# One core of Trainium2: banded attention and a rational-function MLP, with the first tile's loads put first, its masks applied from PSUM and the weights' low bits taken in place

## The chip, the cores and the metric

The kernel runs on one core of one Trainium2 chip. A core has five engines, each with its own queue that it works off in order: TensorE (PE, matrix products, from SBUF into PSUM), VectorE (DVE), ScalarE (ACT), GpSimd (POOL) and SyncE (SP), which here only issues DMA transfers. Engines wait for each other by semaphores. The metric is the device time of one execution in microseconds. Before the change it is 999.59 us, the median of three runs (999.03 to 999.78).

## The reference

Inputs are q, k, v of shape 8 x 8 x 576 x 64 (batch, heads, sequence, head size), w_in 512 x 2048, w_out 2048 x 512, and the coefficients a (four) and b (two).

```
scores = q @ k^T / sqrt(64) - slope[h] * |i - j|       where 0 <= i - j < 128, else -1e9
attn   = exp(scores - max);  attn = attn / (sum + 1e-9)
x      = (attn @ v) as 4608 rows (batch, position) x 512 (head, size)
h      = x @ w_in
g      = (a0 + a1 h + a2 h^2 + a3 h^3) / (1 + |b0| |h| + |b1| h^2 + 1e-6)
out    = g @ w_out
```

All values are float32.

## The kernel before

**Tiles.** The 4608 rows are 36 blocks of 128, two blocks a tile, 18 tiles. For each tile the attention of its 256 rows gives x, the MLP's up-projection runs over 16 chunks c of 128 hidden columns (h), the rational function turns h into g, and the down-projection adds g times the chunk's rows of w_out into two accumulators (acc). Attention comes in half-tiles: step j belongs to tile j // 2 and holds two pairs of heads, i = 0 and 1. Steps 0 and 1 make tile 0's x.

**Attention of one step.** For each pair one DMA brings keys and queries (kq), two bring values (v), all on SP. PE forms scores, those of the window's own positions in a main bank (sc) and the rest in a side bank; DVE merges the two with a predicated copy, then adds the bias and takes the maximum (L507, out pr and st), ACT takes exp (L512), DVE the reciprocal of the sum (L520), POOL multiplies by it (L521). PE transposes pr into PSUM (pt for tile 0, otherwise back into sc), ACT or DVE copies all 512 columns to p_all (L539), and POOL splits what the two blocks of keys share: p_far = p_all times a mask (L543), p_all minus p_far (L544). Then PE multiplies both by v (the values), and ACT or DVE copies the result to x_hi (L413 for tile 0, L415 after).

**Weights.** w_in and w_out arrive as 8-byte words, two 32-bit halves an element; a load brings one chunk of one matrix (raw, 32 loads of 128 x 512 words, in buffers that are later reused). The float32 weight is put together from three results: ACT's Prelu on the upper half (L582), the top three bits of the lower half, taken by ACT or by DVE into the PSUM tile cv (L583), and a shift and an OR on DVE (L584), which gives w32. Tile 0 multiplies in plain float32 with w32. For the later tiles each weight is split into hi, a rounded copy by ACT (L596), and lo, the rest, by DVE or POOL (L597); a product is then three faster matmuls. PSUM holds four buffers under the tag h, shared by h, side, pt, the values' px, cv and the warm-up.

**Rational function.** ACT takes |h| (L635) and a linear term (L638, or L649 after tile 0), POOL forms the denominator (L636 a multiply and add, then a product), ACT logarithm and exp, DVE four or more products (L640 to L647 for tile 0).

**Order.** All work is entered as operations with a due time and the engines that may do it, with a cost in ns for each. A planner (class Plan) goes through time, gives every free engine the ready operation of least due time, and so fixes each engine's queue; the engines then run these queues in order, whatever the real times are. Due times come from one table of numbers (A0, DA, T0, ... in the body of banded_attention_ratio_mlp). The DMA queue of ACT carries the constants (masks16, bias_first, id_sb, bias_std, ab), SP's all other transfers. At the start PE runs seven wide and eight narrow matmuls on constants (L713, L715), before and between the first scores.

Of the kernel before, what the change touches and what calls it, by code (L numbers as in the profile page):

```python
# [79 lines left out]
class Plan:  # L80
# [34 lines left out]
    def order(self):  # L115
# [76 lines left out]
        while n < total:  # L192
# [12 lines left out]
            for e in "pavgsq":  # L205
                while free_at[e] <= t:
# [7 lines left out]
                    if best is None:  # L214
                        break
# [54 lines left out]
def banded_attention_ratio_mlp(ctx: ExitStack, tc: tile.TileContext, kqv, w_in, w_out, ab, bias, ident, out):  # L270
# [87 lines left out]
    def job(j, i):  # L358
# [60 lines left out]
    def attention(j):  # L419
# [4 lines left out]
        side = [slot(ps4, [P, 2, 2, P], F32, f"side{h}", tag="h") for h in range(2)]  # L424
# [6 lines left out]
        extra = lambda h: ap(side[h])[:, 0].rearrange("q i (b c) -> q i b c", b=2)  # L431
# [35 lines left out]
        for h in range(2):  # L467
            plan.op(A + 0.5, {"v": dve(4 * P)}, lambda e, h=h: nc.vector.copy_predicated(
                out=main(h).rearrange("q i b (k c) -> q (i b) k c", k=2),
                mask=halves(ap(masks)[:, 0].bitcast(U32))[:, None].to_broadcast([P, 4, 2, 64]),  # L470
                data=extra(h).rearrange("q i b c -> q (i b) c")[:, :, None].to_broadcast([P, 4, 2, 64])),
                reads=[mk[h], (side[h], 0), (masks, 0)], writes=[mk[h]])
# [10 lines left out]
    def unit(j, i, A, main, mk, pt, v):  # L483
# [54 lines left out]
        plan.op(A + D2, {"p": 28 + 108 * 4}, transpose, reads=[(pr, y) for y in range(4)] + [(id_sb, 0)], writes=pk)  # L538
        plan.op(A + D2 + 0.2, {"a": act(4 * P, 1), "v": dve(4 * P)} if j < 3 else {"a": act(4 * P, 1)}, lambda e: (nc.scalar.copy if e == "a" else nc.vector.tensor_copy)(ap(w)[:, : 4 * P].rearrange("q (k h c) -> q k h c", k=2, h=2), pt()), reads=pk, writes=[(w, 0)])  # L539
        mixed = lambda: ap(w).rearrange("q (k r) -> q k r", k=2)[:, :, : 2 * P].rearrange("q k (h c) -> q k h c", h=2)[:, :, :, :64]  # L540
        far = lambda: ap(masks)[:, 1].rearrange("q (k c) -> q k c", k=2)[:, :, None].to_broadcast([P, 2, 2, 64])
# [20 lines left out]
    def convert(k):  # L562
# [18 lines left out]
        plan.op(T - WL, {"s": 1600}, load, writes=[(raw, 0), (raw, 1)], after=1000 * (T - WL - 4), follows=[raws[k - NL]] if k >= NL else ())  # L581
        plan.op(T, {"a": 575}, lambda e: nc.scalar.activation(top().bitcast(F32), top().bitcast(F32), AF.Prelu, scale=2.0**-112, alpha=-(2.0**32)), writes=[(raw, 0)])  # L582
        plan.op(T, {"a": 640, "v": 603}, lambda e: nc.scalar.activation(cv(), low().bitcast(U32), AF.Relu, bias=low_bias, scale=2.0**-29) if e == "a" else nc.vector.tensor_single_scalar(cv(), low(), 29, op=ALU.logical_shift_right), reads=[(raw, 1)], writes=[ck])  # L583
        plan.op(T + 1, {"v": 603}, lambda e: nc.vector.scalar_tensor_tensor(ap(bits).bitcast(I32), top(), 3, cv(), ALU.logical_shift_left, ALU.bitwise_or), reads=[(raw, 0), ck], writes=[(bits, 0)])  # L584
# [18 lines left out]
    def mlp(t, cs):  # L603
# [32 lines left out]
        plan.op(E, {"g": tsc}, lambda e: nc.gpsimd.tensor_scalar(v(g_q), v(g_u), ap(babs)[:, 1:2], ap(babs)[:, 0:1], ALU.mult, ALU.add), reads=[(g_u, 0), (babs, 0)], writes=[(g_q, 0)])  # L636
# [75 lines left out]
    for j in range(7):  # L712
        plan.op(-9, {"p": 216}, lambda e, j=j: nc.tensor.matmul(ap(warm), ones[:, :P], ones, start=(j == 0), stop=(j == 6)), writes=[(warm, 0)], after=600)  # L713
    for j in range(8):
        plan.op(-9, {"p": 108}, lambda e: nc.tensor.matmul(ap(warm)[:, :256], ones[:, :P], ones[:, :256], start=True, stop=True), writes=[(warm, 0)], after=3617.319 + 500.0 * j)  # L715
# [66 lines left out]
```

## Time and profile before

| | |
|---|---|
| median of three runs | 999.59 us |
| the profiled execution, its time | 999.67 us |
| its span, first to last instruction | 997.9 us |
| busy: PE, DVE, ACT, POOL | 976.8, 791.6, 611.6, 525.4 us |
| mean granted clock of PE | 0.991 |
| moved by DMA | 73.86 MB |

The span is what the trace covers; the execution's own time is 1.8 us more. Two rows of the page show the course, in 40 slices of 25 us, each digit the busy tenths of a slice: PE, and the DMA engines.

```profile
PE   6899899999999999999999999999999999999998
DMA  9991311121112112121212131203021221200000
```

PE is full nearly everywhere but in the first four slices; DMA is full in the first three, while the weights come in. A wait is shown behind a row in square brackets: how long the engine stood idle before it, and who ended that.

### The profile page before, as it was taken

To read this page: it belongs to the slowest core of one execution; us is meant where nothing else is said; L and a number is where in the kernel's file an instruction comes from. 1 tells how busy PE (TensorE), PEld (TensorE's weight loads), DVE (VectorE), ACT (ScalarE), POOL (GpSimd) and SP (SyncE) were. 2 spreads that over 40 slices of the span, in tenths; PEclk is the share of its full clock that TensorE was granted. 3 is DMA by queue.
4 is the path that set the end of the run, shared out by engine and by line. 5 is a ranking of instruction groups with operands and counts; after the bars stand their busy time and mean duration, and the time that the engine had idled before them with its cause. 6 is when DMAs were issued, how large, how long until landed. Compare 5 with 4: busy or idle time off the path is not lost.

```text
span 997.9 us, 25220 instructions
## 1 busy us (share of the span) xinstructions
PE 976.8 (98%) x9999; PEld 867.0 (87%) x9999; DVE 791.6 (79%) x1786; ACT 611.6 (61%) x1410; POOL 525.4 (53%) x529
## 2 busy tenths in 40 slices
PE   6899899999999999999999999999999999999998
PEld 4756698999999999999999999999999999999997
DVE  5799997887878787877787877878787878777775
ACT  5798865665656566655656565656566565656452
POOL 3448984555555554554545454555555545545332
PEclk7899999999999999999999999999999999999999
DMA  9991311121112112121212131203021221200000
GB/s 283 366 325 26 95 48 60 50 94 41 62 51 74 56 54 70 49 75 55 70 49 75 39 96 45 79 2 102 22 80 44 55 75 54 71 1 22 2 22 22
DMA packets 54502, 73.86 MB, mean 74 GB/s; under 512 B 5488, under 2 KB 38512, under 8 KB 54384
## 3 DMA queue, kind: packets, MB, share of 16 engines
q1 hardware_dynamic: 53664, 71.59, 22.9%
q8 instruction: 79, 1.29, 0.6%
q10 hardware_dynamic: 720, 0.66, 0.2%
q14 instruction: 39, 0.32, 0.1%
HBM read 62.79 MB, written 9.44 MB: 72 GB/s over the span
## 4 chain that ended last, share of the span: by engine, by line
PE 91%; DVE 3%; DMA 3%; ACT 1%; issue 1%; SPq 0%; ACTq 0%; DVEq 0%
PE h L621 40%; PE acc L676 39%; PE side L397 5%; PE sc L536 3%; PE sc L444 3%; PE side L444 1%; DMA v<-in_kqv 1%; DVE w L584 1%; DMA kq<-in_kqv 1%; DMA raw<-in_w_in 1%; DMA bias_std<-in_bias 1%; ACT pr L512 0%; DVE cv L583 0%; DVE g_q L644 0%; DVE g L647 0%
## 5 line engine op out<-in xcount | busy, mean ns | idle before, releaser
L621 PE MATMUL h<-x_hi,hi 128*128 128x256 f32 x1088 | 313.6, 288 | 0.0
L621 PE MATMUL h<-x_hi,lo 128*128 128x256 f32 x1088 | 306.2, 281 | 0.0
L621 PE MATMUL h<-x_lo,hi 128*128 128x256 f32 x1088 | 306.0, 281 | 0.0
L636 POOL TENSOR_SCALAR g_q<-g_u,babs 128x512 f32<-128x512 f32 x144 | 123.2, 855 | 252.8 <-ACT g_u L635 252.1
L621 PEld LDWEIGHTS h<-x_lo,hi 128*128 128x128 f32 x1088 | 204.7, 188 | 43.1 <-issue 1.0
L621 PEld LDWEIGHTS h<-x_hi,hi 128*128 128x128 f32 x1088 | 205.3, 189 | 25.4 <-issue 0.7
L676 PE MATMUL acc<-lo,g_h 128*128 128x512 f32 x544 | 214.7, 395 | 0.0
L676 PE MATMUL acc<-hi,g_h 128*128 128x512 f32 x544 | 214.5, 394 | 0.0
L676 PE MATMUL acc<-hi,g_l 128*128 128x512 f32 x544 | 207.7, 400 | 0.0
L621 PEld LDWEIGHTS h<-x_hi,lo 128*128 128x128 f32 x1088 | 204.9, 188 | 0.0
L650 POOL TENSOR_TENSOR g_q<-g_q,g_u 128x512 f32<-128x512 f32 x136 | 175.9, 1293 | 11.0
L521 POOL TENSOR_TENSOR pr<-pr,st 128x512 f32<-128x512 f32 x72 | 76.0, 1055 | 178.8 <-DVE st L520 128.6
L656 DVE SCALAR_TENSOR_TENSOR g_h<-h,ab_sb,g_u 128x512 fp32r<-128x512 f32 x136 | 101.9, 749 | 80.4 <-ACT g_u L654 79.4
L653 ACT ACTIVATE g_u<-g_q,fixed 128x512 f32<-128x512 f32 x136 | 98.0, 720 | 90.8 <-POOL g_q L650 90.7
L512 ACT ACTIVATE pr<-pr,st 128x128 f32<-128x128 f32 x288 | 112.6, 392 | 48.7 <-DVE st L507 48.7
L635 ACT ACTIVATE g_u<-h 128x512 f32<-128x512 f32 x144 | 86.0, 597 | 59.6 <-PE h L621 56.2
L649 ACT ACTIVATE g_p<-h,ab_sb 128x512 f32<-128x512 f32 x136 | 105.5, 778 | 18.0 <-PE h L621 17.9
L651 DVE TENSOR_TENSOR g_p<-h,g_p 128x512 f32<-128x512 f32 x136 | 93.7, 689 | 27.2 <-ACT g_p L649 23.4
L657 DVE SCALAR_TENSOR_TENSOR g_q<-g_q,g_h 128x512 f32<-128x512 f32 x136 | 97.7, 718 | 12.8
L658 DVE SCALAR_TENSOR_TENSOR h<-h,ab_sb,g_q 128x512 f32<-128x512 f32 x136 | 102.9, 756 | 3.5
L676 PEld LDWEIGHTS acc<-hi,g_h 128*128 128x128 f32 x544 | 102.6, 189 | 2.1
L652 DVE SCALAR_TENSOR_TENSOR h<-g_p,ab_sb,h 128x512 f32<-128x512 f32 x136 | 102.1, 751 | 2.5 <-ACT g_u L635 0.3
(75 smaller groups left out, 1516.6 us busy)
## 6 DMA issues: line engine op xcount, KB each, us to landing
kq<-in_kqv SPq DMA_DIRECT2D x72, 320.0 KB, 3.8
v<-in_kqv SPq DMA_DIRECT2D x144, 128.0 KB, 3.9
out<-o SPq DMA_DIRECT2D x34, 256.0 KB, 2.0
raw<-in_w_in SPq DMA_DIRECT2D x16, 512.0 KB, 8.6
raw<-in_w_out SPq DMA_DIRECT2D x16, 512.0 KB, 8.6
bias_t<-in_bias SPq DMA_DIRECT2D x44, 64.0 KB, 2.0
out<-o SPq DMA_DIRECT2D x4, 128.0 KB, 1.8
bias_first<-in_bias ACTq DMA_DIRECT2D x1, 256.0 KB, 4.6
```

Of the source, the lines that this page charges most:

```text
L512: nc.scalar.activation(ap(pr)[:, :, y, :], ap(pr)[:, :, y, :], AF.Exp, bias=ap(st)[:, y : y + 1], scale=-1.0, accum_out=ap(st)[:, 4 + y : ...
L621: nc.tensor.matmul(h(n), w[:, k, :], x[:, k, :], start=(k == 0 and m == 0), stop=(k == NKC - 1 and m == len(seq) - 1))
L636: plan.op(E, {"g": tsc}, lambda e: nc.gpsimd.tensor_scalar(v(g_q), v(g_u), ap(babs)[:, 1:2], ap(babs)[:, 0:1], ALU.mult, ALU.add), reads=[ ...
L649: plan.op(E, {"a": act(W, 1, 2) - 20}, lambda e: nc.scalar.activation(v(g_p), v(h_s), AF.Identity, bias=ap(ab_sb)[:, 2:3], scale=ap(ab_sb) ...
L650: plan.op(E, {"g": ttc}, lambda e: nc.gpsimd.tensor_tensor(v(g_q), v(g_q), v(g_u), ALU.mult), reads=[(g_q, 0), (g_u, 0)], writes=[(g_q, 0) ...
L651: plan.op(E, {"v": dve(W)}, lambda e: nc.vector.tensor_tensor(v(g_p), v(h_s), v(g_p), ALU.mult), reads=[(h_s, 0), (g_p, 0)], writes=[(g_p, ...
L652: plan.op(E, {"v": dve(W, 1)}, lambda e: stt(v(h_s), v(g_p), ap(ab_sb)[:, 1:2], v(h_s), ALU.add, ALU.mult), reads=[(h_s, 0), (g_p, 0), (ab ...
L653: plan.op(E, {"a": act(W, 0, 1)}, lambda e: nc.scalar.activation(v(g_u), v(g_q), AF.Ln, bias=guard, scale=1.0), reads=[(g_q, 0)], writes=[ ...
L656: plan.op(E, {"v": dve(W, 1)}, lambda e: stt(v(g_h), v(h_s), ap(ab_sb)[:, 0:1], v(g_u), ALU.add, ALU.mult), reads=[(h_s, 0), (g_u, 0), (ab ...
L657: plan.op(E, {"v": dve(W)}, lambda e: stt(v(g_q), v(g_q), GUARD, v(g_h).bitcast(F32), ALU.add, ALU.mult), reads=[(g_q, 0), (g_h, 0)], writ ...
L658: plan.op(E, {"v": dve(W, 1)}, lambda e: stt(v(h_s), v(h_s), ap(ab_sb)[:, 0:1], v(g_q), ALU.add, ALU.subtract), reads=[(h_s, 0), (g_q, 0), ...
L676: nc.tensor.matmul(ap(accs[t][i]), x[:, sl], w, start=(c == 0 and part == 0 and m == 0), stop=(c == NFC - 1 and part == parts - 1 and m == ...
```

## The change

Four things are done, and the table of due times is new.

1. *Loads of tile 0 first.* All four kq and then all eight v loads of tile 0 are put ahead of every other transfer of SP; tile 1's kq and v move behind five weight loads. On ACT's DMA queue bias_std goes ahead of id_sb. The two side banks of step 0 are used by step 1 too, in their other half.
2. *Masks from PSUM.* For steps 0 to 4 (DIRECT = 5) ACT copies only half of the transposed columns (L566), and DVE makes the other two products straight from PSUM: p_all times the new mask `near`, which is the far mask with its column halves swapped (L567), and p_far (L568). POOL does neither. In steps 0 and 1 the multiplication by st may go to DVE (L541).
3. *TensorE's gaps filled.* The fifteen warm-up matmuls become as many narrow ones as the planner finds idle time for, from 0.6 to 24.352 us.
4. *Low bits in place.* The lower halves are reduced to their top bits where they lie, by POOL (minimum and multiply) or by ACT (L611); cv and its PSUM buffers go, and DVE's shift and OR (L612) reads both operands from SBUF.

In tile 1 ACT may also do the denominator's multiply and add.

```diff
+DIRECT = 5
...
                     if best is None:
-                        break
+                        if e != "p" or self.fill is None or not self.fill[0] <= t < self.fill[1] or self.fill[2].turn is None:
+                            break
+                        o, spot = Op(), self.fill[2]
+                        o.due, o.engines, o.emit, o.after, o.rows, o.sb = 0.0, {"p": 108}, self.fill[3], 0.0, 1.0, False
...
-    A0, DA, T0, L0, L1 = -4.313, 1.223, 17.768, 62.357, 26.153
+    A0, DA, T0, L0, L1 = -15.22, 0.8197, 19.751, 66.839, 26.934
...
+        for k in range(2):
+            c, o = slice(64 * k, 64 * k + 64), slice(64 - 64 * k, P - 64 * k)
+            plan.op(-7, {"v": 140}, lambda e, c=c, o=o: nc.vector.tensor_copy(ap(near)[:, c], ap(masks16)[:, 1, o]), reads=[(masks16, 0)], writes=[(near, k)])
...
-        plan.op(u0 - JL, {"s": 1.6 * N}, lambda e: eng[e].dma_start(ap(kq), src[:, :N]), writes=[(kq, 0)], after=late)
+        plan.op(u0 - JL if t else 2 * j + i - 19, {"s": 1150}, lambda e: eng[e].dma_start(ap(kq), src[:, :N]), writes=[(kq, 0)], after=late)
...
+        if j < DIRECT:
...
+            plan.op(T, {"a": act(2 * P, 1)}, lambda e: nc.scalar.copy(fresh(1), picked(1)), reads=pk, writes=[(w, 1)])
+            plan.op(T, {"v": dve(2 * P)}, lambda e: nc.vector.tensor_tensor(fresh(0), picked(0), sides(ap(near)), ALU.mult), reads=pk + [(near, 0), (near, 1)], writes=[(w, 0)])
+            plan.op(T, {"v": dve(2 * P)}, lambda e: nc.vector.tensor_tensor(ap(w2), picked(0), sides(ap(masks)[:, 1]), ALU.mult), reads=pk + [(masks, 0)], writes=[(w2, 0)])
...
-        cv_s = slot(ps4, [P, DM], I32, "cv", tag="h")
...
-        plan.op(T, {"a": 640, "v": 603}, lambda e: nc.scalar.activation(cv(), low().bitcast(U32), AF.Relu, bias=low_bias, scale=2.0**-29) if e == "a" else nc.vector.tensor_single_scalar(cv(), low(), 29, op=ALU.logical_shift_right), reads=[(raw, 1)], writes=[ck])
-        plan.op(T + 1, {"v": 603}, lambda e: nc.vector.scalar_tensor_tensor(ap(bits).bitcast(I32), top(), 3, cv(), ALU.logical_shift_left, ALU.bitwise_or), reads=[(raw, 0), ck], writes=[(bits, 0)])
+        plan.op(T, {"g": 880, "a": 690}, lambda e: nc.scalar.activation(low(), low().bitcast(U32), AF.Relu, bias=low_bias, scale=2.0**-29) if e == "a" else nc.gpsimd.tensor_scalar(low(), low().bitcast(U32), 7.49 * 2.0**29, 2.0**-29, ALU.min, ALU.mult), reads=[(raw, 1)], writes=[(raw, 1)])
+        plan.op(T + 1, {"v": 603}, lambda e: nc.vector.scalar_tensor_tensor(ap(bits).bitcast(I32), top(), 3, low(), ALU.logical_shift_left, ALU.bitwise_or), reads=[(raw, 0), (raw, 1)], writes=[(bits, 0)], sb=True)
...
+        plan.op(E, {"g": tsc, "a": act(W, 0, 2) - 20} if t == 1 else {"g": tsc},
...
+    plan.fill = (600, 1000 * FE, warm, warming)
```

SP's queue from its first transfer, before and then after (kq and v are loads of attention, raw loads of weight words, an x behind a row counts repeats):

```order
L374 DMA kq<-in_kqv 128x640 x3
L372 DMA v<-in_kqv 64x2x256 x2
L374 DMA kq<-in_kqv 128x640
L372 DMA v<-in_kqv 64x2x256 x2
L374 DMA kq<-in_kqv 128x640 x2
L372 DMA v<-in_kqv 64x2x256 x2
L577 DMA raw_207<-in_w_in 128x4x256
L372 DMA v<-in_kqv 64x2x256 x6
L577 DMA raw_292<-in_w_in 128x4x256
L577 DMA raw_300<-in_w_in 128x4x256
L577 DMA raw_316<-in_w_in 128x4x256
```

```order
L391 DMA kq<-in_kqv 128x640 x4
L389 DMA v<-in_kqv 64x2x256 x8
L605 DMA raw_265<-in_w_in 128x4x256
L605 DMA raw_276<-in_w_in 128x4x256
L605 DMA raw_283<-in_w_in 128x4x256
L605 DMA raw_295<-in_w_in 128x4x256
L605 DMA raw_305<-in_w_in 128x4x256
L391 DMA kq<-in_kqv 128x640 x2
```

Two kq and four v loads of tile 1 that stood ahead of the third w_in load stand behind the fifth now.

DVE's queue after the change, from the reciprocal of step 1's first pair to the word of chunk 4 (w_c_m is chunk c of w_in for m = 0; pt holds transposed columns):

```order
L540 RECIPROCAL st<-st 128x4
L541 TENSOR_TENSOR pr<-pr,st 128x512
L612 SCALAR_TENSOR_TENSOR w_0_0_410<-raw_265 128x512
L539 TENSOR_TENSOR st<-st,fixed 128x4
L540 RECIPROCAL st<-st 128x4
L541 TENSOR_TENSOR pr<-pr,st 128x512
L567 TENSOR_TENSOR p_all<-pt,near 128x2x2x64
L568 TENSOR_TENSOR p_far<-pt,masks 128x256
L612 SCALAR_TENSOR_TENSOR w_1_0_447<-raw_276 128x512
L612 SCALAR_TENSOR_TENSOR w_2_0_455<-raw_283 128x512
L567 TENSOR_TENSOR p_all<-pt,near 128x2x2x64
L568 TENSOR_TENSOR p_far<-pt,masks 128x256
```

The words of chunks 0 to 2 stand between the last masks of tile 0; before, each of them had its cv operation ahead of it on DVE and the masks were on POOL.

ACT's queue after the change, up to the copies of step 1's x (px), which complete tile 0:

```order
L431 COPY x_hi<-px_371 128x2x128
L431 COPY x_hi<-px_374 128x2x128
L566 COPY p_all<-pt 128x2x2x64
L610 ACTIVATE raw_283<-raw_283 128x512
L610 ACTIVATE raw_295<-raw_295 128x512
L566 COPY p_all<-pt 128x2x2x64
L610 ACTIVATE raw_305<-raw_305 128x512
L431 COPY x_hi<-px_480 128x2x128
L431 COPY x_hi<-px_483 128x2x128
```

The Prelu of the fifth w_in load stands ahead of the last two copies.

More of the change, by code (lines that the diff above doesn't have):

```diff
@@ L91, in __init__ @@
     def __init__(self, slack):
-        self.ops, self.last, self.readers, self.slack = [], {}, {}, slack
+        self.ops, self.last, self.readers, self.slack, self.fill = [], {}, {}, slack, None
     def op(self, due, engines, emit, reads=(), writes=(), after=0.0, follows=(), rows=1.0, sb=False):
@@ L214, in order @@
                     if best is None:
-                        break
+                        if e != "p" or self.fill is None or not self.fill[0] <= t < self.fill[1] or self.fill[2].turn is None:
+                            break
+                        o, spot = Op(), self.fill[2]
+                        o.due, o.engines, o.emit, o.after, o.rows, o.sb = 0.0, {"p": 108}, self.fill[3], 0.0, 1.0, False
+                        o.deps, o.slots, o.users, o.follows, o.engine, o.left = set(), [spot], [], (), e, 0
+                        spot.left.append(o)
+                        spot.open += 1
+                        best = [t, 0.0, 0, o]
+                        ready[e].append(best)
+                        n -= 1
                     o = best[3]
@@ L312, in banded_attention_ratio_mlp @@
     masks = slot(const, [P, 2, P], F32, "masks")
+    near = slot(const, [P, P], F32, "near")
     masks16 = slot(sb3, [P, 2, P], BF16, "masks16", tag="p_far")
@@ L350, in a_time @@
             return A0 + 4 * DA * j
+        if t == 1:
+            return B2 if j == 2 else B3
         m0, m1 = m_time(t - 1, 0), m_time(t, 0)
@@ L423, in attention @@
         back = j - 1 if j > 2 else None
-        side = [slot(ps4, [P, 2, 2, P], F32, f"side{h}", tag="h") for h in range(2)]
+        if j != 1:
+            shared[:] = [slot(ps4, [P, 2, 2, P], F32, f"side{h}", tag="h") for h in range(2)]
+        side, n = list(shared), 1 if j == 1 else 0
         if j == 1:
@@ L430, in attention @@
             main, mk = (lambda h: ap(sc)[:, h]), [(sc, 0), (sc, 1)]
-        extra = lambda h: ap(side[h])[:, 0].rearrange("q i (b c) -> q i b c", b=2)
+        extra = lambda h: ap(side[h])[:, n].rearrange("q i (b c) -> q i b c", b=2)
         if j < NJ:
@@ L447, in attention @@
             for i in range(2):
-                plan.op(A + DU * i, {"p": 290 + 664}, lambda e, i=i: scores(i), reads=jobs[i][3], writes=mk + [(side[0], 0), (side[1], 0)], rows=0.9)
+                plan.op(A + DU * i, {"p": 290 + 664}, lambda e, i=i: scores(i), reads=jobs[i][3], writes=mk + [(side[0], n), (side[1], n)], rows=0.9)
         else:
@@ L471, in attention @@
                 data=extra(h).rearrange("q i b c -> q (i b) c")[:, :, None].to_broadcast([P, 4, 2, 64])),
-                reads=[mk[h], (side[h], 0), (masks, 0)], writes=[mk[h]])
+                reads=[mk[h], (side[h], n), (masks, 0)], writes=[mk[h]])
         for i in range(2):
@@ L635, in mlp @@
         plan.op(E, {"a": act(W, 1)}, lambda e: nc.scalar.activation(v(g_u), v(h_s), AF.Abs), reads=[(h_s, 0)], writes=[(g_u, 0)])
-        plan.op(E, {"g": tsc}, lambda e: nc.gpsimd.tensor_scalar(v(g_q), v(g_u), ap(babs)[:, 1:2], ap(babs)[:, 0:1], ALU.mult, ALU.add), reads=[(g_u, 0), (babs, 0)], writes=[(g_q, 0)])
+        plan.op(E, {"g": tsc, "a": act(W, 0, 2) - 20} if t == 1 else {"g": tsc},
+                lambda e: nc.scalar.activation(v(g_q), v(g_u), AF.Identity, bias=ap(babs)[:, 0:1], scale=ap(babs)[:, 1:2]) if e == "a" else nc.gpsimd.tensor_scalar(v(g_q), v(g_u), ap(babs)[:, 1:2], ap(babs)[:, 0:1], ALU.mult, ALU.add),
+                reads=[(g_u, 0), (babs, 0)], writes=[(g_q, 0)])
         if whole:
@@ L711, in banded_attention_ratio_mlp @@
     ones = nc.const_aps.tensor(1.0, [P, 512], BF16)
[L712 to L715, printed above, removed]
+    warming = lambda e: nc.tensor.matmul(ap(warm)[:, :256], ones[:, :P], ones[:, :256], start=True, stop=True)
+    plan.op(-30, {"p": 108}, warming, writes=[(warm, 0)], after=600)
+    plan.op(-30, {"p": 108}, warming, writes=[(warm, 0)], after=1000 * FE)
+    plan.fill = (600, 1000 * FE, warm, warming)
     for j in range(3):
```

41 lines of the change are left out of this document (24 added, 17 removed).

## The prediction

> **What bounds the kernel now.** I read the busy times by stretch first, because the end of a stretch tells who was late in it. The columns are the stretch, its length, busy time of TensorE (PE), its weight loads, VectorE (DVE), ScalarE (ACT) and GpSimd (POOL) with instruction counts, the granted clock, the DMA share and GB/s.
>
> ```profile
> 0.00:33.40 33.40, 21.79 (x359) 16.62 (x360) 19.30 (x83) 18.56 (x65) 13.62 (x20) 0.74 1.01 301
> 33.40:111.30 77.90, 73.58 (x538) 51.57 (x539) 72.28 (x143) 68.73 (x143) 48.74 (x46) 1.00 0.62 208
> 111.30:180.00 68.70, 67.40 (x755) 60.31 (x754) 60.37 (x128) 44.12 (x104) 47.10 (x42) 1.00 0.23 72
> 180.00:940.00 760.00, 760.00 (x8024) 690.54 (x8023) 599.74 (x1376) 454.94 (x1061) 396.97 (x404) 1.00 0.18 55
> 940.00:998.00 58.00, 54.06 (x330) 47.95 (x329) 39.96 (x59) 25.23 (x40) 18.95 (x18) 1.00 0.05 19
> ```
>
> From 180 to 940 us PE is never idle at full clock: there is nothing to win there, only to lose. The end has the same PE order before and after from the last tile's first chunks on. So a gain must come out of the first 111 us. There the first 33 us are start-up (clock 0.74, DMA share 1.01), and in the next 77.9 PE, DVE and ACT are all near full. The timeline of PE gives the two ends of that second stretch and the price of each kind of work (start, length, operation, idle before it):
>
> ```profile
> 33.42 1.10 PE L621 MATMUL h<-x_hi,w 128*128 128x256 f32 x4 [1.29 <-DVE x_hi L413]
> 34.79 4.48 PE L621 MATMUL h<-x_hi,w 128*128 128x256 f32 x20
> 39.20 0.67 PE L397 MATMUL side<-p_all,v 64*64 64x128 f32 x16
> ...
> 40.59 0.40 PE L444 MATMUL sc<-kq 64*64 64x128 f32 x8
> ...
> 42.04 1.13 PE L621 MATMUL h<-x_hi,w 128*128 128x256 f32 x4
> ...
> 52.00 0.60 PE L536 MATMUL sc<-id_sb,pr 128*128 128x128 f32 x4
> 52.43 0.60 PE L621 MATMUL h<-x_hi,w 128*128 128x256 f32 x2
> 52.87 1.02 PE L676 MATMUL acc<-w,g 128*128 128x512 f32 x2
> 53.73 1.03 PE L621 MATMUL h<-x_hi,w 128*128 128x256 f32 x4
> ...
> 107.64 3.70 PE L676 MATMUL acc<-w,g 128*128 128x512 f32 x8 [1.06 <-DVE g L647]
> ```
>
> At 33.42 PE gets the first tile's last x and starts its up-projection in earnest; at 107.64 + 3.70 = 111.3 its last down-projection ends. By starts, an up matmul of tile 0 (two records) takes (39.20 - 34.79) / 10 = 0.44 us, a down matmul 0.86, a group of four transposes 0.43, the values of one half-tile 1.39, its scores 1.45. A group of three for tile 1 costs 0.36, by this row of the chain of waits, 48 in 5.76:
>
> ```profile
> 957.58 5.76 PE h L621 x48
> ```
>
> **The sum.** Between the two ends the old order holds 62 up matmuls (27.3), 32 down (27.5), 24 groups of tile 1 (8.6), 5 groups of transposes (2.2), two values (2.8) and two scores (2.9): 71.3 us of work in 77.9, so 6.6 of waiting. The new order, counted between the same two events, has 21 groups of tile 1 and otherwise the same: 70.2. Three groups and one of transposes come after it instead, 1.5 us.
>
> When can the new one start? This is the main term. Before, the third w_in word load landed at about 23.7:
>
> ```profile
> 23.68 0.68 ACT L582 ACTIVATE raw<-raw 128x512 f32<-128x512 f32 x1 [0.31 <-DMA raw<-in_w_in]
> 24.26 0.63 ACT L413 COPY x_hi<-px 128x256 f32<-128x256 f32 x2
> ```
>
> The sizes stand in the list of DMA issues:
>
> ```profile
> kq<-in_kqv SPq DMA_DIRECT2D x72, 320.0 KB, 3.8
> v<-in_kqv SPq DMA_DIRECT2D x144, 128.0 KB, 3.9
> ...
> raw<-in_w_in SPq DMA_DIRECT2D x16, 512.0 KB, 8.6
> ```
>
> SP had issued 6 kq, 12 v and 3 raw up to it: 1920 + 1536 + 1536 = 4992 KB. The queue is saturated there, so a transfer's place in bytes is its time. In the new order the fifth w_in load ends 4 kq, 8 v and 5 raw: 1280 + 1024 + 2560 = 4864 KB, so it too lands at about 23.7. ScalarE's new queue holds the last two x copies of tile 0 right behind that load's Prelu, so they can't be earlier: 23.7 + 0.57 + 0.63 (rows above, the Prelu by start to start) = 24.9, and PE starts at **25.0**. The attention itself asks for about the same: its last masks on DVE stand behind the third word load, 3840 KB, at the 301 GB/s of the first stretch 3.9 us before 4992 KB; then come a conversion, two masks and the values, some 3.5 us. That is 8.4 us earlier than 33.4, and no earlier, though all of tile 0's scores could be there by 10 us.
>
> If waiting stays 6.6, the last down matmul ends at 25.0 + 70.2 + 6.6 = 101.8 and the shift is 111.3 - 101.8 - 1.5 = **8.0 us**. Why should waiting stay? These are the loads of the three helpers between the same ends.
>
> - DVE, 72.3 before. These rows price the edits: L583 in that stretch (DVE, then ACT), L597 (DVE, then POOL), and an operation of the masks' size:
>
> ```profile
> 33.40:111.30 77.90, 9.48 (x14) 9.04 (x13) 1.00 0.62 208
> 33.40:111.30 77.90, 5.70 (x5) 16.70 (x13) 1.00 0.62 208
> L416 DVE TENSOR_TENSOR x_lo<-side,x_hi 128x256 fp32r<-128x256 f32 x68 | 25.8, 418 | 0.3 <-ACT x_hi L415 0.2
> ```
>
> The 14 conversions on L583 leave (-9.5), four lo subtractions (5.70 for five, -4.6) and four operations of tile 1 (4 x 0.7, -2.8) move elsewhere; eight masks of 256 elements out of PSUM come, priced by the x_lo row, also 256 out of PSUM (+3.3), and two predicated copies and four maxima of one more attention (+2.5): 61.2.
> - ACT, 68.7: thirteen L583 operations fewer, seven in place more, 0.70 each: 64.6.
> - POOL, 48.7: four mask pairs (-6.3) and three lo (-3.9) leave, 20 conversions come.
>
> ```profile
> L636 POOL TENSOR_SCALAR g_q<-g_u,babs 128x512 f32<-128x512 f32 x144 | 123.2, 855 | 252.8 <-ACT g_u L635 252.1
> L543 POOL TENSOR_TENSOR p_far<-p_all,masks 128x256 f32<-128x256 f32 x72 | 61.3, 852 | 10.6 <-ACT p_all L539 9.3 <-DVE p_all L539 1.0
> L650 POOL TENSOR_TENSOR g_q<-g_q,g_u 128x512 f32<-128x512 f32 x136 | 175.9, 1293 | 11.0
> L597 POOL TENSOR_TENSOR lo<-w,hi 128x512 fp32r<-128x512 f32 x21 | 27.6, 1342 | 1.0 <-ACT hi L596 0.9
> ```
>
> No row shows POOL on integer words at a stride. Its bounds are the L636 row, 0.86, the same operation, and the L597 row, 1.34, two operands. I take 0.86, the like form: 38.5 + 17.2 = 56 of 77 us; at 1.34 it is 65. Both fit; the dearer one delays g_q, which stands behind conversions in POOL's queue, and I keep 3 us of extra waiting for it in the range.
>
> So DVE and ACT get lighter, POOL heavier. I leave the waiting where it was, with 2 to 11 us as its ends. The two small edits have these covers:
>
> ```profile
> 6.47 0.73 PE L715 MATMUL warm<-const-bfloat16-1.0 128*128 128x256 bf16 x5
> 7.13 0.45 PE L444 MATMUL sc<-kq 64*64 64x128 f32 x8
> 6.59 1.50 DVE L468 COPY_PREDICATED sc<-masks,side 128x512 f32<-128x512 uint32 x2 [1.86 <-PE side L444]
> ```
>
> The matmuls that fill PE's gaps cost nothing: they end at 24.35 by the plan's own limit, where PE waits for x anyway; each is at most 0.13 (five start within 0.66 us). If the attention were ready earlier, they would hold PE until then, at most 1 us. Keeping the clock up shortens transposes and values that stand in front of x, but x is set by the landing. The two column swaps of the mask, two DVE copies of 64 columns, lie in DVE's wait for scores before 6.6 us.
>
> One cost lies behind the stretch. POOL now makes 24 of the 32 lo tiles instead of 21, and from the first to the last its queue holds 23 x 1.34 + 7 x 1.29 + 11 smaller operations (10.0) = 49.8 us against about 52 of PE work, which was the same before with two lo fewer. It is covered, by little.
>
> **A rule against this change.** L612 on DVE now has both inputs in SBUF, where cv was in PSUM. What the trace shows of such an operation (L657) beside POOL:
>
> ```profile
> 140.71 0.74 POOL L543 TENSOR_TENSOR p_far<-p_all,masks 128x256 f32<-128x256 f32 x1 [1.75 <-ACT p_all L539]
> 140.75 1.25 DVE L657 SCALAR_TENSOR_TENSOR g_q<-g_q,g_h 128x512 f32<-128x512 f32 x1
> ...
> 208.39 1.28 POOL L636 TENSOR_SCALAR g_q<-g_u,babs 128x512 f32<-128x512 f32 x1 [0.23 <-ACT g_u L635]
> ...
> 208.33 0.69 DVE L657 SCALAR_TENSOR_TENSOR g_q<-g_q,g_h 128x512 f32<-128x512 f32 x1
> ```
>
> Behind a POOL TENSOR_TENSOR, DVE waited 0.56 longer; ahead of a TENSOR_SCALAR, POOL waited 0.5. DVE beginning in the middle of a TENSOR_SCALAR is not in the trace; its price lies between 0 and 0.86. The Trainium skill, page "SBUF — State Buffer", section "Who interferes with whom", says that a VectorE instruction with two SBUF inputs contends with any GpSimd instruction that reads SBUF, and that whoever is first holds the port for its whole instruction. By that rule every conversion can stop L612, and the trace agrees for the two cases it has.
>
> **Rivals.**
> - *DVE and POOL pace each other.* 27 operations of L612 in the stretch at 0.56 to 0.77 each add 15 to 21 us to DVE's 61, so 76 to 82, more than PE's 70.2. With the old 6.6 of waiting the stretch takes 83 to 89 and the shift is 3 us to below nothing, as it was 8.4 + 77.9 - 1.5 - stretch: **998**. For it: DVE queues are in order and POOL's share is over 70%. Against it: all 27 would have to meet POOL at work; with POOL reading two thirds of the time and half an operation left on average it is 27 x 0.67 x 0.4 = 7 us, and DVE stays at 68.
> - *The attention does not come first after all.* L612 for the first words stands on DVE ahead of the last two multiplications by st and of the last masks. Before, the fourth w_in load was issued here:
>
> ```profile
> 20.25 1.89 SPq L577 DMA_DIRECT2D raw<-in_w_in  x2
> ```
>
> If the fifth is held on SP to that moment and takes the 8.6 us that the list gives, it lands at 28.9, PE starts at 30.2 and the shift is 2.8: **996.9**. Against it: it is SP's 17th issue now, and the old 17th, a v load, is the fourth of the six in the row below and went out near 14; with 8.6 us that is 22.6, close to the 23.7 by bytes.
>
> ```profile
> 11.20 4.84 SPq L372 DMA_DIRECT2D v<-in_kqv  x6
> ```
> - *Slower: the new steady order.* The due times are new for all tiles. In the new order 17 down matmuls and a block of values and scores follow each other without an up matmul. The nearest wait beside such a block:
>
> ```profile
> 43.74 4.99 PE L621 MATMUL h<-x_hi,w 128*128 128x256 f32 x22 [0.56 <-DVE x_lo L416]
> ```
>
> Two blocks a tile and 15 tiles at 0.56 make 16.8 us: 991.7 + 16.8 = **1008.5**. It turns the gain into a loss from 0.53 us a tile on. Against it: DVE is busy for only 79% there (599.7 of 760), and PE's work per tile is the same.
>
> **The numbers.** The profiled execution took 999.67, its span 997.9; the median of the runs is 999.59, 0.1 lower, which I ignore. 999.67 - 8.0 = **991.7**. Chances: forecast 0.60 (987 to 996 by its waits), pacing 0.20 (half of it within 0.2%), late attention 0.10, slower steady state 0.10. 0.2%, 2.0 us, is about what a measurement of this kernel tells from no change. Faster 0.78, the same 0.10, slower 0.12. The range, 986.5 to 999.5, leaves out the slower case and a tail below.
>
> **What would show it.** Right: the up matmuls run from 25 us on, the last tile-0 down matmul ends near 102, PE is full from 180 on, L612 stays near 0.75. Wrong: L612 or L611 well above 1 us; x copies of tile 0 done after 28; a fifth w_in load that lands much later than 23.7; PE idle per tile after 180; or PE waits for g (L677) of 10 us and more in the stretch.

## The result and the profile after

The changed kernel takes **1008.19 us**, the median of four runs (1008.09 to 1008.88), beside 999.55 (999.03 to 999.78) for the kernel before on the same chip: a ratio of 1.0089, 95% interval 1.0071 to 1.0106. That is 8.6 us slower where I forecast 8 us faster, and outside my range. The profiled execution took 1008.10 us, its span is 1006.3, which is 8.4 more than the 997.9 of before.

The busy times by stretch of the kernel after, cut at the two events of the prediction (PE begins behind tile 0's last x; the last down matmul of tile 0 ends). Columns as there: PE, weight loads, DVE, ACT, POOL, clock, DMA share, GB/s.

```profile
0.00:26.30 26.30, 25.37 (x394) 20.21 (x394) 15.40 (x66) 13.35 (x47) 11.37 (x10) 1.00 0.92 286
26.30:119.10 92.80, 76.60 (x593) 53.07 (x593) 70.63 (x155) 65.05 (x148) 89.90 (x55) 0.96 0.64 202
119.10:180.00 60.90, 60.40 (x716) 54.22 (x715) 55.12 (x119) 46.02 (x104) 47.79 (x41) 1.00 0.18 55
180.00:940.00 760.00, 760.00 (x8028) 690.61 (x8027) 592.25 (x1382) 447.57 (x1067) 389.79 (x403) 1.00 0.19 57
```

The start is 7.1 us earlier (26.3 for 33.4), as meant. From 180 to 940 us PE is full, as before. The whole loss lies between: the stretch takes 92.8 us instead of 77.9, so 14.9 - 7.1 = 7.8 of the span's 8.4 us. PE is idle for 16.2 us of it (92.80 - 76.60; before 77.90 - 73.58 = 4.3), and POOL is busy for 89.90 of 92.80. The bound of this stretch is now POOL. Whom PE waited for there (total, times, longest):

```profile
PE sc L556 <- POOL pr L541: 10.5, 3, 6.4
PE acc L706 <- DVE g L677: 2.5, 1, 2.5
```

The new operation on POOL and its user on DVE, as groups over the whole span (count, busy, mean ns, idle before):

```profile
L611 POOL TENSOR_SCALAR raw<-raw 128x512 int32<-128x512 uint32 x25 | 57.8, 2312 | 4.2 <-DMA raw<-in_w_in 2.3
```

A conversion in place takes 2.31 us on POOL, not the 0.86 that I took, nor the 1.34 that I called its upper bound. How that becomes a wait of PE is seen in the timelines of DVE, POOL and PE around the longest one (start, length, operation, idle before):

```profile
47.42 0.16 DVE L540 RECIPROCAL st<-st 128x4 f32<-128x4 f32 x1
...
46.37 10.11 POOL L611 TENSOR_SCALAR raw<-raw 128x512 int32<-128x512 uint32 x4
56.56 1.04 POOL L541 TENSOR_TENSOR pr<-pr,st 128x512 f32<-128x512 f32 x1
...
57.65 1.12 PE L556 MATMUL sc<-id_sb,pr 128*128 128x128 f32 x4 [6.40 <-POOL pr L541]
58.56 1.06 PE L649 MATMUL h<-x_hi,w 128*128 128x256 f32 x2
```

At 47.6 everything that the multiplication by st needs is there. But it stands behind four conversions in POOL's queue, which the planner had priced at 880 ns each, and they end at 56.5. PE, whose queue has the transposes next, stands still for 6.4 us. The transposes and matmuls behind the wait then run at half speed (1.12 us for 0.66; 1.06 for 0.60): the granted clock was 1.00 from 40 to 50 us, 0.81 from 50 to 60 and 0.85 from 60 to 70.

### The profile page after: what moved, and what is told of

It is laid out like the page before. It is cut to its first block, busy times and chain, and to the rows that moved or that the text cites. A ratio compares the mean times of both kernels' runs of the same rounds, so it can differ in the third digit from the quotient of the medians.

```text
span 1006.3 us, 25442 instructions
## 1 busy us (share of the span) xinstructions
PE 984.9 (98%) x10100; PEld 873.4 (87%) x10100; DVE 779.8 (77%) x1788; ACT 602.0 (60%) x1411; POOL 561.6 (56%) x528
## 4 chain that ended last, share of the span: by engine, by line
PE 92%; DMA 3%; POOL 1%; ACT 1%; DVE 1%; issue 1%; POOLq 0%; DVEq 0%
PE h L649 39%; PE acc L706 39%; PE side L415 5%; PE sc L464 3%; PE sc L556 3%; PE warm L742 2%; PE side L464 2%; DMA kq<-in_kqv 1%; DMA v<-in_kqv 1%; DMA raw<-in_w_out 1%; POOL raw L611 1%; DMA bias_t<-in_bias 1%; ACT raw L610 0%; DVE w L612 0%; PE px L415 0%
## 5 line engine op out<-in xcount | busy, mean ns | idle before, releaser
L665 POOL TENSOR_SCALAR g_q<-g_u,babs 128x512 f32<-128x512 f32 x138 | 113.5, 823 | 222.0 <-ACT g_u L663 221.7
L706 PE MATMUL acc<-hi,g_l 128*128 128x512 f32 x544 | 199.9, 401 | 0.0
L680 POOL TENSOR_TENSOR g_q<-g_q,g_u 128x512 f32<-128x512 f32 x136 | 179.2, 1318 | 8.4
L541 POOL TENSOR_TENSOR pr<-pr,st 128x512 f32<-128x512 f32 x69 | 75.7, 1097 | 159.5 <-issue 97.1
L683 ACT ACTIVATE g_u<-g_q,fixed 128x512 f32<-128x512 f32 x136 | 98.2, 722 | 105.2 <-POOL g_q L680 105.2
L706 PEld LDWEIGHTS acc<-lo,g_h 128*128 128x128 f32 x544 | 102.1, 188 | 6.6
L706 PEld LDWEIGHTS acc<-hi,g_l 128*128 128x128 f32 x544 | 99.3, 189 | 6.7
```

The source lines that it names most:

```text
L541: plan.op(A + 1.2, {"g": 185 + 1.6 * 4 * P, "v": dve(4 * P)} if j < 2 else {"g": 185 + 1.6 * 4 * P}, lambda e: eng[e].tensor_tensor(ap(pr) ...
L665: lambda e: nc.scalar.activation(v(g_q), v(g_u), AF.Identity, bias=ap(babs)[:, 0:1], scale=ap(babs)[:, 1:2]) if e == "a" else nc.gpsimd.te ...
L680: plan.op(E, {"g": ttc}, lambda e: nc.gpsimd.tensor_tensor(v(g_q), v(g_q), v(g_u), ALU.mult), reads=[(g_q, 0), (g_u, 0)], writes=[(g_q, 0) ...
L683: plan.op(E, {"a": act(W, 0, 1)}, lambda e: nc.scalar.activation(v(g_u), v(g_q), AF.Ln, bias=guard, scale=1.0), reads=[(g_q, 0)], writes=[ ...
L706: nc.tensor.matmul(ap(accs[t][i]), x[:, sl], w, start=(c == 0 and part == 0 and m == 0), stop=(c == NFC - 1 and part == parts - 1 and m == ...
```

## The experiments

Three theories. **A**: the price of a conversion on POOL is the loss. **B**: the operation itself is cheap, and VectorE's L612 holds it up. **C**: the early order is at fault, whatever the price.

**The same order, other words (e1).**

```diff
-nc.gpsimd.tensor_scalar(low(), low().bitcast(U32), 7.49 * 2.0**29, 2.0**-29, ALU.min, ALU.mult)
+nc.gpsimd.tensor_scalar(low().bitcast(F32).rearrange("p (b c) -> p b c", b=4),
+    ap(masks).rearrange("p i c -> p (i c)").rearrange("p (c w) -> p c w", w=2)[:, :, 0][:, None].to_broadcast([P, 4, P]),
+    0.0, 0.0, ALU.min, ALU.mult)
```

> The changed kernel in its own order on every engine; only the 25 conversions on POOL read a float32 tile (the masks, at the same step of 8 bytes) and write float32 zeros to the same words, so the weights lose their three lowest bits. Theory A (the price of a conversion on POOL, 2.0 to 2.5 us where I had 0.86, is the whole loss): the operation takes 0.8 to 0.9, PE's waits for pr and g in the first 120 us shrink from 19 us to about 6, time 992 to 996. Theory B (the operation is as cheap as I said and VectorE's L612, with two inputs in SBUF, holds it up): L612 is still there, so 2.0 to 2.5 us each and 1008. Theory C (the early order is at fault, whatever the price): the operation is cheap and the time still above 1003.

Measured: 999.61 us (998.5 to 1002.19, ten runs), ratio 1.001 (1.000 to 1.002). The group of this operation:

```profile
L611 POOL TENSOR_SCALAR raw<-masks 128x512 f32<-128x512 f32 x25 | 52.0, 2105 | 3.2 <-DMA raw<-in_w_in 3.0 <-DMA raw<-in_w_out 0.2
```

No theory had this: A and C expected a cheap operation, and B, which has the price right, a time of 1008. Float32 words are hardly cheaper, so the type is not what costs. Yet 5.8 us less on POOL (52.0 for 57.8) took 8.6 us from the span (997.7 for 1006.3), and PE's waits for pr in the stretch fell from 10.5 to 2.0 us: POOL is so full that its time is the kernel's, and more. C cannot be read from this run, since the operation didn't become cheap.

**No conversion on POOL (e2), and a planner that knows the price (e3).**

For e2 the engines and the operation are exchanged, for e3 one number:

```diff
-{"g": 880, "a": 690}
+{"v": 603, "a": 690}
...
-nc.gpsimd.tensor_scalar(low(), low().bitcast(U32), 7.49 * 2.0**29, 2.0**-29, ALU.min, ALU.mult)
+nc.vector.tensor_single_scalar(low(), low(), 29, op=ALU.logical_shift_right)
```

```diff
-{"g": 880, "a": 690}
+{"g": 2500, "a": 690}
```

> The changed kernel with the conversions in place on VectorE (a shift of the integer words, 17 of them) and ScalarE (15), none on POOL; the planner orders anew. A: DVE carries 17 x 0.65 = 11 us more than in the forecast (61 to 72, as much as before), POOL's queue is free, PE's waits near the old 6.6: 992 to 998. B: the same or a little better, so it doesn't part A from B. C: above 1003.

> The changed kernel with one number changed: the planner's cost of a conversion on POOL, 880 to 2500 ns. It then puts 14 on POOL instead of 25, 18 on ScalarE, and orders around them. A: 14 x 2.45 = 34 us on POOL instead of 61; time 996 to 1003. B: each conversion still waits behind L612 in the same way, 14 of them, 1002 to 1006. C: 1008.

Measured: e2 1000.18 us (998.90 to 1001.41), ratio 1.001 (1.0001 to 1.0019); e3 999.81 us (999.07 to 1001.21), ratio 1.001 (1.000 to 1.002). Both get rid of the loss and neither wins anything; e3 is where A had it (996 to 1003), e2 is not (992 to 998). In e3's profile PE waits for pr only 1.3 us; 4.7 of its 8.8 us of idle time between 26 and 106 us is one gap before L415 that the trace puts down to no engine ("issue"). The windows of e2 from 40 to 100 us:

```profile
40.00:60.00 20.00, 16.95 (x137) 11.14 (x139) 19.16 (x35) 19.02 (x37) 6.88 (x8) 0.91 1.07 331
60.00:80.00 20.00, 18.15 (x109) 11.97 (x100) 20.00 (x44) 15.64 (x34) 7.01 (x6) 1.00 1.02 291
80.00:100.00 20.00, 19.62 (x206) 13.89 (x205) 19.69 (x44) 16.44 (x42) 16.32 (x14) 1.00 0.23 69
```

DVE (third figure) is busy for 58.9 of 60 us and POOL nearly free at first: the load went to the engine that the change was to relieve. These two runs leave C alive: perhaps the early order is worth nothing. What was missing was a cheap conversion on POOL, so I measured the operation by itself.

**The operation alone (e4, e6).** Both append operations on POOL to the changed kernel, behind its end. X holds a weight load's words, Y is another buffer of that size; far takes every second word, near2 the first 512. Of e4's nine forms, three, written out:

```diff
+    for k in range(3):
+        nc.gpsimd.tensor_scalar(far(Y), far(X).bitcast(U32), 7.49 * 2.0**29, 2.0**-29, MIN, MUL)
...
+    for k in range(3):
+        nc.gpsimd.tensor_scalar(near2(Y), near2(X).bitcast(U32), 7.49 * 2.0**29, 2.0**-29, MIN, MUL)
...
+    for k in range(3):
+        nc.gpsimd.tensor_scalar(far(Y).bitcast(F32), far(Y).bitcast(F32), 7.49, 2.0, MIN, MUL)
```

> The changed kernel with 27 operations on POOL behind its end, when VectorE has nothing to do: minimum and product of 512 words per partition in nine forms, three each: unsigned to signed words, unsigned words to float32, float32 to signed words, float32 to float32, at a step of 8 bytes and contiguous, and in place. A: the form of the change takes 1.9 to 2.1 us with VectorE idle; if the step makes it, float32 at that step takes as long and the contiguous words 0.8; if the types make it, the contiguous words take 1.9 to 2.1 too and float32 0.8 at either step. B: all of them 0.8 to 0.9. The total time says nothing here.

Four of the nine groups of e4 (all nine have a mean of 1917 to 1961 ns):

```profile
L779 POOL TENSOR_SCALAR probe_hi<-probe_hi 128x512 int32<-128x512 uint32 x3 | 5.9, 1961 | 14.2 <-DMA probe_hi<-in_w_out 14.0
L787 POOL TENSOR_SCALAR probe_hi<-probe_hi 128x512 f32<-128x512 f32 x3 | 5.9, 1961 | 0.2
...
L781 POOL TENSOR_SCALAR probe_hi<-probe_hi 128x512 int32<-128x512 uint32 x3 | 5.8, 1917 | 0.2
...
L789 POOL TENSOR_SCALAR probe_hi<-probe_hi 128x512 f32<-128x512 f32 x3 | 5.8, 1917 | 0.2
```

The first two are at a step of 8 bytes, the last two contiguous; whole numbers and float32 in each case. With VectorE idle the form of the change takes 1.96, so B falls as the main cause, and neither type nor step matters. What is left is the pair of operations, minimum and product.

In e6 the form stays and the pair changes, ts standing for the first line above up to the numbers:

```diff
+    for k in range(3):
+        ts(2.0**-29 - 2.0**-49, 2.0**-20 - 0.5, MUL, ADD)
...
+    for k in range(12):
+        nc.vector.scalar_tensor_tensor(Z[:, :DM], far(X, 1), 3, far(X), ALU.logical_shift_left, ALU.bitwise_or)
+    for k in range(6):
+        ts(7.49 * 2.0**29, 2.0**-29, MIN, MUL)
```

> The changed kernel with operations on POOL behind its end: the form of the change with eight pairs of operations, three each, VectorE idle (minimum and product; product and sum with immediate numbers; the same with numbers from a tile; minimum and product with numbers from a tile; product and minimum; maximum and product; product alone; minimum alone). Then six of minimum and product beside twelve of L612's form on VectorE, and six of product and sum beside the same. If the pair makes the price: product and sum 0.8 in both, all others 1.9. If the immediate numbers do: 0.8 for both pairs with numbers from a tile, 1.9 else. Beside VectorE: 2.4 to 2.5 if each conversion waits for one of L612, 1.96 if VectorE waits instead. The total time says nothing here.

The rows of e6, on POOL and DVE (several operations of one pair are merged in a row, or two pairs where no other operand parts them):

```profile
1008.10 6.05 POOL L776 TENSOR_SCALAR probe_hi<-probe_hi 128x512 int32<-128x512 uint32 x3 [13.75 <-DMA probe_hi<-in_w_out]
...
1008.10 8.21 POOL L776 TENSOR_SCALAR probe_hi<-probe_hi 128x512 int32<-128x512 uint32 x6 [13.75 <-DMA probe_hi<-in_w_out]
1016.41 2.57 POOL L776 TENSOR_SCALAR probe_hi<-probe_hi,ab_sb 128x512 int32<-128x512 uint32 x3
...
1019.08 6.53 POOL L776 TENSOR_SCALAR probe_hi<-probe_hi,ab_sb 128x512 int32<-128x512 uint32 x3
...
1025.70 6.06 POOL L776 TENSOR_SCALAR probe_hi<-probe_hi 128x512 int32<-128x512 uint32 x3
...
1029.80 8.10 POOL L776 TENSOR_SCALAR probe_hi<-probe_hi 128x512 int32<-128x512 uint32 x4
...
1025.70 21.87 POOL L776 TENSOR_SCALAR probe_hi<-probe_hi 128x512 int32<-128x512 uint32 x12
...
1047.81 9.92 DVE L795 SCALAR_TENSOR_TENSOR probe_hi<-probe_hi 128x512 int32<-128x512 int32 x12
1047.86 14.03 POOL L776 TENSOR_SCALAR probe_hi<-probe_hi 128x512 int32<-128x512 uint32 x6 [0.29 <-DVE probe_hi L793]
...
1062.13 10.54 DVE L800 SCALAR_TENSOR_TENSOR probe_hi<-probe_hi 128x512 int32<-128x512 int32 x12
1062.18 6.32 POOL L776 TENSOR_SCALAR probe_hi<-probe_hi 128x512 int32<-128x512 uint32 x6 [0.29 <-DVE probe_hi L798]
```

Three of minimum and product take 6.05 us, 2.0 each; the next three, product and sum, fill the rest of the 8.21, 0.72 each with the gaps. With numbers from a tile the two pairs take 6.53 / 3 = 2.18 and 2.57 / 3 = 0.86, so immediate numbers are not the cause. Product and minimum takes 6.06 / 3 = 2.02, maximum and product the same (four in 8.10, the last of the one and all of the other); product alone and minimum alone share what is left of the twelve, (21.87 - 12.12) / 6 = 1.6 (by windows of their own, 4.76 us for three of the one and 4.75 for three of the other). Even one operation alone is not cheap. Of the forms tried only product and sum is, which is L665's pair (L636 in the kernel before), the row that I had priced by.

Beside VectorE, which works on L612's form for the first 9.9 of the 14.03 us, the first four conversions take 9.94 us, 2.48 each against 2.0 alone; the last two, with VectorE done, take 2.0 again. Product and sum takes 6.32 / 6 = 1.05 against 0.72. VectorE pays too: 0.83 each beside the conversions and 0.98 beside product and sum (5.87 for six), against 0.73 by start to start once POOL is done. So B has a part: of the mean of 2.31 in the kernel some 0.3 is over the 2.0 of the operation alone, and the pair makes the rest.

**The price that the forecast assumed (e5).** Product and sum can do the conversion too: the word times 2^-29, less almost a half, rounds to the three top bits.

```diff
-nc.gpsimd.tensor_scalar(low(), low().bitcast(U32), 7.49 * 2.0**29, 2.0**-29, ALU.min, ALU.mult)
+nc.gpsimd.tensor_scalar(low(), low().bitcast(U32), 2.0**-29 - 2.0**-49, 2.0**-20 - 0.5, ALU.mult, ALU.add)
```

> The changed kernel in its own order on every engine; the 25 conversions on POOL use product and sum (2^-29, then a little less than -0.5) in place of minimum and product, so with the same words, types and step they still take the three highest of the low bits. If the pair of operations makes the price (A: every one of the nine forms with minimum and product took 1.92 to 1.96 us, while product and sum takes 0.77 to 0.86 on L665), a conversion takes 0.8 to 1.3 and POOL's load in the stretch falls from 97% to about 75%. Then my forecast is tried for the first time with the price it assumed: A says 991 to 995. C (the early order keeps PE waiting for other reasons too) says 996 to 1000, about what the kernels with 2.0 us or without POOL conversions gave (999.6, 1000.2). If immediate numbers make the price and not the pair, it stays 2.0 to 2.5 and the time near 1000 to 1008.

Measured: **994.0 us** (992.71 to 994.39, five runs) beside 999.7, ratio 0.9941 (0.9927 to 0.9954); span 992.5. In A's range, outside C's. One pair of operations in one instruction, with every queue in the same order, is worth 14.2 us (1008.2 - 994.0). This version beats both kernels. Its groups, windows, waits and two rows of PE:

```profile
L611 POOL TENSOR_SCALAR raw<-raw 128x512 int32<-128x512 uint32 x25 | 20.9, 838 | 21.4 <-DMA raw<-in_w_in 14.2 <-DMA raw<-in_w_out 6.3
```

```profile
0.00:26.00 26.00, 24.98 (x392) 20.14 (x392) 16.64 (x67) 13.47 (x47) 6.04 (x10) 1.00 0.89 278
26.00:105.20 79.20, 74.34 (x593) 52.60 (x593) 70.33 (x155) 64.50 (x148) 57.68 (x54) 0.98 0.78 240
```

```profile
PE acc L706 <- DVE g L677: 3.0, 1, 3.0
PE side L415 <- issue: 1.8, 1, 1.8
```

```profile
44.45 5.40 PE L706 MATMUL acc<-w,g 128*128 128x512 f32 x8 [3.02 <-DVE g L677]
...
104.29 1.02 PE L706 MATMUL acc<-w,g 128*128 128x512 f32 x2
```

The waits for pr are gone. PE's idle time in the stretch is 4.9 us, about what it was before.

**The low bits alone (e7, e8).** In the kernel before, only the lines of the conversion are exchanged for the new ones, first with minimum and product (e7), then with the exchange of e5's diff (e8).

```diff
-{"a": 640, "v": 603}, lambda e: nc.scalar.activation(cv(), low().bitcast(U32), AF.Relu, bias=low_bias, scale=2.0**-29)
+{"g": 880, "a": 690}, lambda e: nc.scalar.activation(low(), low().bitcast(U32), AF.Relu, bias=low_bias, scale=2.0**-29)
...
-nc.vector.tensor_single_scalar(cv(), low(), 29, op=ALU.logical_shift_right)
+nc.gpsimd.tensor_scalar(low(), low().bitcast(U32), 7.49 * 2.0**29, 2.0**-29, ALU.min, ALU.mult)
...
-top(), 3, cv(), ALU.logical_shift_left, ALU.bitwise_or
+top(), 3, low(), ALU.logical_shift_left, ALU.bitwise_or
```

> The kernel before with one part of the change alone: conversions in place, on POOL (minimum and product, 18 of them) or ScalarE (14), the planner's numbers otherwise as before, so no early attention and no masks by VectorE. A: 18 x 2.0 to 2.5 us come on a POOL that keeps its mask products too (48.7 + 40 of 78 us), so PE waits for pr and g: 1004 to 1012. C: the part does no harm by itself, 998 to 1001.

> The kernel before with the conversions in place, as in the run of this part alone that took 1019.4 us, but with product and sum in place of minimum and product; the order is the same as in that run. If the pair's price is the loss there too: 18 operations of 0.7 to 0.85 instead of 2.13, 23 us less on POOL, and the time falls by 15 to 20 us, to 999 to 1004. If in-place conversion hurts for another reason (a wait for the word loads in POOL's queue, or the port beside VectorE), it stays above 1008.

Measured: e7 1019.37 us (1018.2 to 1020.0), ratio 1.0197 (1.0183 to 1.0211); e8 1001.7 us (999.94 to 1002.72), ratio 1.0029 (1.0019 to 1.0038). e7 was dearer than A's 1004 to 1012. Its group and the two largest waits of PE up to 200 us:

```profile
L580 POOL TENSOR_SCALAR raw<-raw 128x512 int32<-128x512 uint32 x18 | 38.3, 2130 | 4.7 <-DMA raw<-in_w_in 3.3
```

```profile
PE sc L536 <- POOL pr L521: 7.5, 3, 4.5
PE px L397 <- POOL p_all L544: 6.4, 2, 4.8
```

Here POOL still makes the masks' products (L544), and those are delayed as well as pr. With the cheap pair the same order loses 17.7 us of that, and what stays is a part that by itself gives nothing, 2.6 us slower than before (1001.7 beside 999.1). So the 5.7 us that e5 wins come, as far as the parts add up, from the rest of the change: the early attention, the masks by VectorE, the fills and the new table, which weren't taken apart further, except for one.

**The fills (e9) and the planner's number (e10).** e9 is e5 without most of the fills; e10 is e5 with the planner's price of a conversion at 690 instead of 880.

```diff
+        fills = [o for o in order if o.emit is warming]
         for o in order:
-            o.emit(o.engine)
+            if o not in fills[22:-1]:
+                o.emit(o.engine)
```

> The changed kernel with product and sum (994.0 us) and all but the first 22 and the last of the 116 small matmuls that fill PE's gaps left out; every other instruction in the same order. My forecast gave the fills no gain and no cost: by it 994 again, within 1. If the clock that they keep at 1.00 through the first 25 us is worth something, scores, transposes and values of the first tile run at half speed and PE's first up matmul comes 1 to 3 us later than 27.5: 995 to 998.

> The changed kernel with product and sum, and the planner told the price that the trace shows for it, 690 ns instead of 880. If the planner's numbers now fit the chip, the order loses a part of the 5 us that PE still waits between 26 and 105 us: 990 to 994. If the price was near enough, 993 to 995. Above 996 the old number was right by luck only.

Measured: e9 996.53 us (993.33 to 1001.71, twelve runs), ratio 0.9978 (0.9960 to 0.9997). Its profiled execution has a start at clock 0.93 instead of 1.00, and yet it had tile 0's x earlier (the last copies end at 25.4 us, in e5 at 25.8):

```profile
0.00:26.00 26.00, 17.27 (x346) 13.38 (x347) 16.73 (x67) 13.38 (x47) 5.70 (x10) 0.93 0.89 279
```

```profile
24.93 0.45 PE L464 MATMUL sc<-kq 64*64 64x128 f32 x8
...
30.32 0.21 PE L464 MATMUL side<-kq 64*64 64x64 f32 x1 [4.16 <-issue]
```

The scores that follow the values begin at 24.93; in e5 they begin at 26.0, behind seven fills of 0.96 us in all. So the fills cost up to 1.1 us at that place. Later PE loses 4.2 us to something that the trace does not show, and its next up matmul comes at 30.8, late through this gap. Gaps of this kind ("issue") add up to 8.0 us between 26 and 110 us here and to 1.8 in e5: more than the 4.5 us by which this execution's span is longer. It is one of the longer runs of e9 (998.78). Six of the twelve took 993.3 to 995.4 us, the other six 997.7 to 1001.7, while those of e5 spread over 1.7. Whether the fills are worth 2 us, or only make the time steadier, and what makes the gaps, stays open.

e10: 996.91 us, ratio 0.9982 (0.9973 to 0.9991; one of eleven runs took 2316 us, for no reason that I know). Above 996, which I had put down as "right by luck": the true price makes an order that is 2.9 us slower than the one made with 880 (by their ratios to the kernel before, 0.9982 and 0.9941). Perhaps the table of due times fits the old number only; that is not shown.

## Why the prediction was wrong

The terms of my sum, against the kernel after and against e5, which has the price that I assumed. Waiting is the idle time of PE in the windows (before: 4.3).

| | forecast | after | e5 |
|---|---|---|---|
| PE begins behind tile 0's x, us | 25.0 | 26.3 | 26.0 |
| one conversion on POOL, us | 0.86 | 2.31 | 0.84 |
| POOL busy in the stretch, us | 56 | 89.9 | 57.7 |
| ACT busy | 64.6 | 65.1 | 64.5 |
| DVE busy | 61.2 | 70.6 | 70.3 |
| PE waits | as before | 16.2 | 4.9 |
| length of the stretch | 76.8 | 92.8 | 79.2 |
| its end | 101.8 | 119.1 | 105.2 |
| time | 991.7 | 1008.2 | 994.0 |

**The step that failed** is this one: "No row shows POOL on integer words at a stride. Its bounds are the L636 row, 0.86, the same operation, and the L597 row, 1.34, two operands. I take 0.86, the like form". I looked for what could make the words dear, their type and their step, and both turned out to cost nothing. I passed over what differs in the arithmetic: L636 multiplies and adds, the conversion takes a minimum and multiplies. The instruction's name is the same, TENSOR_SCALAR; the price is not. So 1.34 was no upper bound, and my sentence "Both fit" held only inside a bound that no row gave. The trace could have told from which price it fails: POOL's other work was 38.5 us by my own sum, so twenty conversions in a stretch of 76.8 fill POOL at 38.3 / 20 = 1.9 us each. With that worked out, the slower side would have had a rival of its own, in which POOL becomes the bound. The one I gave it, a wait per block in the steady order, was the wrong mechanism: PE is full from 180 to 940 us.

**How it spread**: not through g_q, as I feared for the dear end, but above all through pr (10.5 of PE's 16.2 us), which stands in the same queue.

**What held.** The landing: the fifth w_in load was there at 22.6 in the kernel after, and at 23.4 in e5, for 23.7 forecast:

```profile
22.64 0.70 ACT L610 ACTIVATE raw<-raw 128x512 f32<-128x512 f32 x1 [0.29 <-DMA raw<-in_w_in]
25.43 0.65 ACT L431 COPY x_hi<-px 128x256 f32<-128x256 f32 x2 [2.08 <-PE px L415]
```

But the x copies waited for the values, not for that load. It was the attention's own chain that ended last, which I had put at about the same time: the copies end at 26.1 (25.8 in e5) where I had 24.9, and seven fills behind the values hold PE until 26.3 and 26.0, the first row. What begins there are the scores of step 2, so the up matmuls, which I had from 25 us on, follow at 27.8 (27.5 in e5). My count "and otherwise the same" was wrong as well. In the kernel before, step 2's scores ran at 13.6 to 16.3 us, while PE waited for x; now their kq loads stand behind five weight loads, and the stretch holds three blocks of scores, not two (96 of these matmuls into the main banks, 64 before). That is 1.45 us of work that the sum lacks.

ACT's load held, and POOL's at the assumed price (56 against 57.7). DVE got 9 us more than I said: L612 took 23.9 us for 27 operations in e5's stretch, not 18.2; the rest is in maxima (24 where I had counted 20), masks (10 for 8), one lo tile and the small operations on st. With the price set right, the rest of the sum is off by 2.3 us (994.0 for 991.7): 1.0 from the start, 1.45 from the scores and some 1.7 because eight down matmuls behind a 3.0 us wait ran slower (5.40 us for the 3.70 of before, at a granted clock of 0.68); other terms, which I have not followed, take back 1.9.

**The rule on the shared port.** Of my pacing rival a part came true: L612 got dearer by 0.2 us each, where the rival had 0.56 to 0.77. (Its better end was 84.8 - 82.6 = 2.2 us of gain, not the 3 that I wrote.) POOL paid as well: 2.48 for 2.0 beside L612's form, 1.05 for 0.72. The rule of the Trainium skill that I named ("SBUF — State Buffer", "Who interferes with whom") foresees that either side can be held up, and the runs agree. It was about a fifth of what POOL's operation cost over my price: (2.31 - 2.0) of (2.31 - 0.86).

The Trainium skill, page "GPSIMD Engine Reference", section "3.1 Elementwise — side-by-side cycle accounting", gives 769 ns as measured for a tight loop over 512 elements, and calls it the best case. The runs agree for product and sum (0.72 to 0.86) and show 1.6 to 2.2 alone for every other operation or pair tried, so a best case is no price for an operation that isn't in the trace.

## What to carry to other kernels

An instruction's name is not its price: bound a new operation by rows with the same arithmetic on the same engine, and where there is none, work out from which price its engine becomes the bound, and give that case its chance. Work that is early enough for everyone can still do harm in an in-order queue, by standing in front of what PE needs next. And a loss of 14 us can hang on one pair of operations: before a change is dropped, try the same step in the cheap form that the engine's other rows show.

## What the hardware showed unexpectedly

- POOL's TENSOR_SCALAR over 128 x 512 words takes 0.7 to 0.9 us for product and sum, and 2.0 to 2.2 for minimum and product in either order or maximum and product. One operation alone takes 1.6, twice the price of product and sum together. Type (unsigned, signed, float32), a step of 8 bytes, working in place and where the numbers come from change it by 0.2 us at most. Beside VectorE operations with two SBUF inputs it takes 2.48 and 1.05 for minimum and product and for product and sum, against 2.0 and 0.72 alone.
- In e1 the same order and nearly the same price (25 at 2.11 for 2.31, together 5.8 us) gave 8.6 us less: on an engine that is busy for 97% of a stretch, each microsecond saved came back more than once. Most conversions took 2.0 there, as with VectorE idle, while VectorE's L612 took 0.93 us for the 0.85 of the kernel after. So part of the waiting may have gone over to VectorE; the runs do not show why.
